# A decode block with attention on one core: wo in 48 rows per partition, read behind the last V, with attention outputs placed by selector matmuls, batch outermost and q by columns

## The chip, the cores and the metric

One core of one Trainium2 chip runs the kernel. The metric is the device time of one execution in microseconds (us); lower is better. The engines are PE (TensorE, matmuls; PEld is its weight load), DVE (VectorE), ACT (ScalarE), POOL (GpSimd) and SP (SyncE, which here only issues DMA transfers). A trace of one execution with its profile was taken for every kernel. Times in the profile count from the span's start; the timed runs are longer than the span.

A ratio below is the mean time of one kernel's fast runs over that of the other's of the same rounds, so it is not quite the ratio of the medians that are quoted.

## The reference, cut to what matters

One decode step for four sequences: layer norm, attention over a cache of 4096 positions with 32 heads of 192 values, then a gated feed-forward layer.

```python
B, Sq, D = 4, 1, 640
Hq, Hkv, Sk, Dh = 32, 32, 4096, 192          # every head has its own K and V
F = 1536
q = layernorm(x) @ wq                         # wq [640, 6144]
scores = einsum("bhqd,bhkd->bhqk", q, k_cache) * Dh ** -0.5
o = einsum("bhqk,bhkd->bhqd", softmax(scores), v_cache)
h = x + o.reshape(B, Sq, Hq * Dh) @ wo        # wo [6144, 640]
g = silu(layernorm(h) @ w_gate); u = layernorm(h) @ w_up
out = h + (g * u) @ w_down
# ... all inputs bf16
```

K and V are 201 MB each. They are read once and hardly reused, so the reading is the job.

## The kernel before

The work is cut into 32 units of one batch and four heads. Per unit there is one K of 6.29 MB and one V of 6.29 MB, each read by one DMA transfer with one contiguous run of 49152 bytes per partition. The engines work in order: four DVE products of K with q (`tt`), four PE sums (`red`), four DVE sums (`rsum`), the maximum, the exponentials on ACT; the PV matmuls of the unit before are put in front of the last `red`.

```python
def src(a, u):
    c, b = u // B, u % B                      # heads outermost, batch innermost
    return a[b, 4 * c:4 * c + 4].rearrange("h (q t) d -> (h q) (t d)", t=T)

def load_k(u):                                # two K slots
    deps = [lambda: tk["tt", u - 2, NQ - 1]] if u >= 2 else ([wq_used] if u == 1 else [])
    ...
VP = [(0, 64), (64, 96), (96, 112), (112, T)] # the last V comes in four pieces
def load_v(u):                                # one V slot: waits for the PV before
    deps = [(lambda: tk["pv", u - 1]) if u >= 1 else wq_used]
    ...
# one SP queue: wq, K0, K1, V0, K2, V1, K3, ..., K31, V30, wo_a, V31, wo_b, wg, wu, wd
def load_wo(lo, hi, t, deps):                 # three rows of 1280 bytes: runs of 3840 bytes
    a = dma("sp", lambda e: e.dma_start(
        t[:, :, :, :].rearrange("q p j n -> q p (j n)"),
        wo[lo * 2 * DH:hi * 2 * DH, :].rearrange("(p q j) n -> q p (j n)", q=128, j=3)), ...)
# ...
def o_t(u):                                   # transposes one unit's output: 6 fp32 matmuls
    for j in range(3):
        for s in range(2):
            lo = XO.start + 2 * j
            op("pe", lambda e, j=j, s=s, lo=lo: e.matmul(
                psL[64 * s:64 * s + 64, lo:lo + 2], lhsT=orow[:, j:DH:3], rhs=pick[:, s:4:2], ...))
# ... otm divides by the softmax sum; the 144 matmuls of wo_a run before the last PV
```

Of the kernel before, what the change touches and what calls it, by code (L numbers as in the profile page):

```python
# [12 lines left out]

LOOPS = True
FASTQ = False
LATE = True
SPLITU = True
XONE = False
AHEAD = False
# [17 lines left out]
class Prog:  # L37
# [33 lines left out]
    def roll(self, eng, first, last):  # L71
        self.rolled[eng] = (first, last)
# [14 lines left out]
    def emit(self, block, final):  # L87
# [24 lines left out]
        def run(eng):  # L112
            def body(e):
                ops, waits = self.ops[eng], self.waits(eng)
                if AHEAD and eng in ("dve", "act"):
                    e.addr_align(bass.FETCH_BLOCK_INSTRUCTIONS, offset=64, max_nops=0)
                i = 0
                if eng in self.rolled:
                    first, last = self.rolled[eng]
# [21 lines left out]
                    with self.nc.Fori(0, count, 1, engines=bass.OrderedEngineSet([e.engine]),  # L141
                                      head_slot={e.engine: 0} if eng == "pe" else None) as s:
                        self.shift = s
                        for j in range(n):
                            for k, v, d in plan[j]:
                                e.wait_ge(k, s * d + v)
                            one(e, ops[a + j])
                        self.shift = 0
# [39 lines left out]
def build_kernel(nc: bass.Bass, cfg: Cfg, x, kc, vc, wq, wo, wg, wu, wd, out):  # L188
# [4 lines left out]
    P = H // 2  # L193
    NU = (H // 4) * B
# [3 lines left out]
    J = DH // R  # L198
    QS = 2.0 ** -4
    alpha = 1.0 / (QS * math.sqrt(DH))  # L200
    assert B == 4 and DH == 192 and D == 640 and F == 1536 and P == 16 and T == 128 and QT * R == 512
# [16 lines left out]
    OTall = sb("OTall", [128, NU, 2, 3], BF16)  # L218
    qsb = sb("qsb", [128, 4, 2 * DH], BF16)
    sel = sb("sel", [128, B, 128 if FASTQ else 32], BF16)  # L220
    identF = sb("identF", [128, 128], FP32)
    identH = sb("identH", [128, 128], FP16)
    identB = sb("identB", [128, 128], BF16)
    halfm = sb("halfm", [128, 128], FP32)
# [6 lines left out]
    xrow = x4 = sb("x4", [B, D], BF16) if XONE else sb("xrow", [128, DQ], BF16)  # L231
# [8 lines left out]
    lsb = sb("lsb", [128, 2], FP32)  # L240
    invL = sb("invL", [128, 2], FP32)
# [11 lines left out]
    assert at(vslot) - at(kslot[1]) == SLOT and at(prod[1]) - at(prod[0]) == SLOT // 4  # L253
    WA = 12
    wqsb = nc.alloc_sbuf_tensor_at("wq_sb", [128, CD, H * DH], BF16, offset=at(kslot[1]))
    woA = nc.alloc_sbuf_tensor_at("wo_a", [128, WA, 3, D], BF16, offset=at(kslot[0]))
    woB = nc.alloc_sbuf_tensor_at("wo_b", [128, P - WA, 3, D], BF16, offset=at(prod[0]))
# [5 lines left out]
    psR, psS, psO, psH, psL = PB[0:4], PB[4], PB[5], PB[6], PB[7]  # L263
    psQ = [PB[7], PB[3]]
    XT, XB, XL, XO = slice(0, 128), slice(128, 132), slice(0, 2), slice(4, 10)
# [6 lines left out]

    if XONE:
        xd = [dma("act", lambda e: e.dma_start(x4[:, :], x[:, 0, :]), S_x)]
    else:
        xd = [dma("act", lambda e, n=n: e.dma_start(xrow[32 * n:32 * n + B, :], x[:, 0, n * DQ:(n + 1) * DQ]), S_x)
              for n in range(4)]
# [10 lines left out]
    c3 = op("pool", lambda e: e.memset(halfm[:, :], 0.0), [c2])  # L288
    for r in range(4):
        c3 = op("pool", lambda e, r=r: e.memset(halfm[32 * r:32 * r + 32, 64 * (r % 2):64 * (r % 2) + 64], 1.0), [c3])  # L290
    c4 = op("pool", lambda e: e.memset(ones_row[:, :], 1.0), [c3])
    c4 = op("pool", lambda e: e.memset(lsb[:, :], 0.0), [c4])
    pool_done = op("pool", lambda e: e.memset(pbuf[:, :, :], 0.0), [c4])

    if not XONE:
        zx = op("dve", lambda e: e.memset(xrow[:, :], 0.0))
        for t in xd:
            t.deps.append(zx)
    zp = None
    for k in (6, 0, 1, 2, 3, 5):  # L300
        zp = op("dve", lambda e, k=k: e.memset(PB[k][:, 0:2 * DH], 0.0))
    op("dve", lambda e: e.memset(epsv[:, :], eps))
    if FASTQ:
        ksel = op("dve", lambda e: e.tensor_copy(
            out=sel[:, :, :].rearrange("q b (h i) -> q b h i", h=4),
            in_=identF[:, :].rearrange("q (h r) -> q r h", h=4)[:, 0:B, :, None].broadcast_to([128, B, 4, 32])), [c2])
    else:
        ksel = op("dve", lambda e: e.tensor_copy(
            out=sel[:, :, :], in_=r32[:, 0:B][:, :, None].broadcast_to([128, B, 32])), [c1])
# [5 lines left out]
    kidb = op("dve", lambda e: e.tensor_copy(out=identB[:, :], in_=identF[:, :]), [c2])  # L315
# [21 lines left out]
    if XONE:  # L337
        for n in range(4):
            a = op("pe", lambda e, n=n: e.matmul(psH[32 * n:32 * n + B, 0:DQ], lhsT=identB[0:B, 0:B],
                                                 rhs=x4[:, n * DQ:(n + 1) * DQ], start=True, stop=True), [kidb, zp] + xd)  # L340
        ln1 = layer_norm(psH[:, 0:DQ], [a])
    else:
        ln1 = layer_norm(xrow[:, :], xd)
        for n in range(4):
            op("pe", lambda e, n=n: e.matmul(psH[32 * n:32 * n + B, 0:DQ], lhsT=identB[:, 32 * n:32 * n + B],
                                             rhs=xrow[:, :], start=True, stop=False), [kidb, zp] + xd)
# [5 lines left out]
    if FASTQ:  # L352
        for c in range(CD):
            for k in range(4):
                for n in range(4):
                    rhs = wqsb[:, c, 8 * k * DH:8 * (k + 1) * DH].rearrange("q (s d) -> q s d", s=2)[:, :, n * DH:(n + 1) * DH]
                    mm = partial(held_matmul, size=(128, 32), position=(0, 32 * n)) if k else lambda e, *a, **kw: e.matmul(*a, **kw)
                    a = op("pe", lambda e, k=k, c=c, n=n, rhs=rhs, mm=mm: mm(
                        e, PB[k][32 * n:32 * n + B, 0:2 * DH], lhsT=lnT[:, c, 0:B], rhs=rhs,
                        start=(c == 0), stop=(c == CD - 1)), [ln1, wq_land, zp])  # L360
                if c == CD - 1:
                    qcopy.append(op("act", lambda e, k=k: e.activation(
                        out=qsb[:, k, :], in_=PB[k][:, 0:2 * DH], func=ACTF.Copy, scale=1.0), [a]))
    else:
        for k in range(4):
            for c in range(CD):
                for n in range(4):
                    p = 2 * (4 * (k // 2) + n) + k % 2
                    a = op("pe", lambda e, k=k, c=c, n=n, p=p: e.matmul(  # L369
                        PB[k][32 * n:32 * n + B, 0:2 * DH], lhsT=lnT[:, c, 0:B],  # L370
                        rhs=wqsb[:, c, p * 2 * DH:(p + 1) * 2 * DH], start=(c == 0), stop=(c == CD - 1)),
                        [ln1, wq_land, zp])
            qcopy.append(op("act", lambda e, k=k: e.activation(
                out=qsb[:, k, :], in_=PB[k][:, 0:2 * DH], func=ACTF.Copy, scale=1.0), [a]))
    wq_used = a

    def src(a, u):
        c, b = u // B, u % B
        return a[b, 4 * c:4 * c + 4].rearrange("h (q t) d -> (h q) (t d)", t=T)
# [8 lines left out]
    VP = [(0, 64), (64, 96), (96, 112), (112, T)]  # L388

    def load_v(u):  # L390
        deps = [(lambda: tk["pv", u - 1]) if u >= 1 else wq_used]
        if u < NU - 1:
            landed["v", u] = [dma("sp", lambda e: e.dma_start(  # L393
                vslot[:, :, :].rearrange("q t d -> q (t d)"), src(vc, u)), S_v, deps)]
        else:
            s = src(vc, u).rearrange("q (t d) -> q t d", d=DH)
            landed["v", u] = [dma("sp", lambda e, lo=lo, hi=hi: e.dma_start(vslot[:, lo:hi, :], s[:, lo:hi, :]),
                                  sem(f"s_v{lo}"), deps) for lo, hi in VP]
# [3 lines left out]
    for u in range(NU - 1):  # L402
        load_v(u)
        if u + 2 < NU:
            load_k(u + 2)
    wo_land = {}

    def load_wo(lo, hi, t, deps):
        a = dma("sp", lambda e: e.dma_start(
            t[:, :, :, :].rearrange("q p j n -> q p (j n)"),  # L410
            wo[lo * 2 * DH:hi * 2 * DH, :].rearrange("(p q j) n -> q p (j n)", q=128, j=3)), sem(f"s_wo{lo}"), deps)
        for p in range(lo, hi):
            wo_land[p] = a

    load_wo(0, WA, woA, [lambda: tk["tt", NU - 2, NQ - 1]])
    if LATE:
        load_v(NU - 1)
    load_wo(WA, P, woB, [lambda: tk["red", NU - 1, NQ - 1]])
    if not LATE:
        load_v(NU - 1)  # L420
# [4 lines left out]
    for lo, hi in ((0, 3), (3, CD)) if SPLITU else ((0, CD),):  # L425
# [12 lines left out]
    qbc = {}  # L438
    if FASTQ:
        for i in range(NU // 2):  # L440
            k, b, bank = i // B, i % B, psQ[i % 2]
            a = op("pe", lambda e, bank=bank, k=k, b=b: e.matmul(
                bank[:, 0:2 * DH], lhsT=sel[:, b, :], rhs=qsb[:, k, :], start=True, stop=True),
                [qcopy[k], qcopy[-1], ksel, qbc.get(i - 2)])
            qbc[i] = op("act", lambda e, k=k, b=b, bank=bank: e.activation(
# [119 lines left out]
    for u in range(NU):  # L565
# [12 lines left out]
        if u >= 1:  # L578
            stt(u - 1)
# [113 lines left out]
```

## Time and profile before

The time before was 991.96 us (median of 3 runs, 991.73 to 992.19).

| what | reading |
|---|---|
| busy share of the span | PE 59%, DVE 56%, ACT 11%, DMA queue q1 99.5% |
| bytes read | 424.29 MB |
| rate in the middle | 433 GB/s |
| rate while wo_a is read | 407 GB/s |
| last K usable | 924.54 us |
| last piece of wd usable | 986.91 us |
| end | 990.1 us |

These are the lines of the page: span, busy time of the engines, the DMA queue, and the chain of work that ended last by line.

```profile
span 990.1 us, 9773 instructions
PE 581.2 (59%) x4656; PEld 117.9 (12%) x3248; DVE 552.5 (56%) x451; ACT 108.7 (11%) x348; POOL 3.4 (0%) x19
...
q1 hardware_dynamic: 12752, 424.29, 99.5%
```

The queue is busy for all but 0.5% of the span, so a gain has to come from shorter work on the queue, or from queue time that is lost at the ends.

The windows view gives, for a stretch of time, the busy time of each engine, the granted PE clock, the share of the DMA engines and the rate in GB/s. The first two are stretches of two units in the middle; the third lies inside the reading of wo_a.

```profile
core 0: us, PE busy (x) PEld busy (x) DVE busy (x) ACT busy (x) POOL busy (x), PEclk, DMA share, GB/s
110.49:168.57 58.08, 34.74 (x260) 6.51 (x172) 33.93 (x26) 5.79 (x20) 0.00 (x0) 0.79 1.00 433
865.53:923.61 58.08, 35.01 (x260) 6.51 (x172) 33.94 (x26) 5.79 (x20) 0.00 (x0) 0.79 1.00 433
938.00:950.00 12.00, 8.46 (x101) 2.93 (x83) 5.05 (x8) 3.08 (x11) 0.00 (x0) 0.96 1.02 407
```

The small packets of wo cost 6% of the rate. The share of 1.02 is the sum of the packets' durations, and above 1.00 it says that the durations overlap.

The timeline has start, duration, engine, line and operation; in brackets the idle time before it and what ended it. These two lines mark where the last K has landed (DVE starts on it) and where the last piece of wd has landed (PE loads weights for the last down matmuls).

```profile
924.54 6.63 DVE L468 TENSOR_TENSOR prod<-k,qball 128x6144 f16<-128x6144 bf16 x2 [5.92 <-DMA k<-in_A_k_cache_dram]
...
986.91 0.10 PEld L632 LDWEIGHTS pb<-wd_sb,guT 128*4 128x4 bf16 x8 [0.43 <-DMA wd_sb<-in_B_w_down_dram]
```

I call the time up to the first line the head and the middle, and from the first to the second, 986.91 - 924.54 = 62.37 us, the tail. What is left to the end is 3.2 us.

### The profile page before, as it was taken

The page shows a single profiled execution, that of the slowest core. Times are in us where ns is not written, and L with a number is a line of the kernel's source. Part 1 is how long each engine was busy: PE and PEld are TensorE (multiplying, and loading weights), DVE is VectorE, ACT ScalarE, POOL GpSimd, SP SyncE. Part 2 cuts the span into 40 slices and gives each one's busy share as a digit, 9 for nine tenths or more (in the row PEclk, how much of TensorE's full clock was granted, in tenths as well). Part 3 has the DMA queues.
Part 4 walks back from the last instruction along what each step waited for, and adds up shares of the span by engine and source line. Part 5 has one row for each costly group of instructions (what it writes and reads, how often), then busy time and mean ns, then how long its engine had stood idle before and what let it go on. Part 6 is the DMA issues. An engine that isn't in the chain of part 4 may idle for free.

```text
span 990.1 us, 9773 instructions
## 1 busy us (share of the span) xinstructions
PE 581.2 (59%) x4656; PEld 117.9 (12%) x3248; DVE 552.5 (56%) x451; ACT 108.7 (11%) x348; POOL 3.4 (0%) x19
## 2 busy tenths in 40 slices
PE   0876655666555576555557655555665555666564
PEld 0100111110101111001111100111110011110031
DVE  1486655566645556664555666455666555566602
ACT  0311111110011110001111001111100111100011
POOL 1000000000000000000000000000000000000000
PEclk9797778887777888777788877788887778887765
DMA  9999999999999999999999999999999999999998
GB/s 407 418 443 432 422 445 429 429 445 417 441 435 423 445 429 429 445 419 439 435 423 445 429 429 445 421 437 435 423 445 429 429 445 421 437 433 425 423 417 333
DMA packets 12810, 424.43 MB, mean 429 GB/s; under 512 B 1280, under 2 KB 1280, under 8 KB 4096
## 3 DMA queue, kind: packets, MB, share of 16 engines
q1 hardware_dynamic: 12752, 424.29, 99.5%
q8 instruction: 7, 0.11, 0.0%
q14 instruction: 3, 0.02, 0.0%
q10 hardware_dynamic: 48, 0.01, 0.0%
HBM read 424.29 MB, written 0.01 MB: 429 GB/s over the span
## 4 chain that ended last, share of the span: by engine, by line
DMA 64%; PE 19%; DVE 12%; SPq 2%; issue 1%; ACT 0%; DVEq 0%; ACTq 0%
DMA k<-in_A_k_cache_dram 59%; PE pb L168 12%; DVE prod L468 12%; PE pb L520 4%; DMA wd_sb<-in_B_w_down_dram 2%; DMA xrow<-in_A_x_dram 2%; PE pb L476 2%; SPq L432 1%; PE pb L369 1%; SPq L426 1%; SPq L393 0%; PE pb L456 0%; DVE sc L481 0%; ACT qball L460 0%; SPq L422 0%
## 5 line engine op out<-in xcount | busy, mean ns | idle before, releaser
L468 DVE TENSOR_TENSOR prod<-k,qball 128x6144 f16<-128x6144 bf16 x128 | 426.3, 3351 | 195.6 <-DMA k<-in_A_k_cache_dram 195.6
L168 PE MATMUL pb<-prod,identH 128*128 128x512 f16 x1408 | 385.4, 430 | 0.0
L476 PE MATMUL pb<-prod,identH 128*128 128x512 f16 x128 | 57.7, 450 | 338.2 <-DVE prod L468 330.2
L481 DVE TENSOR_REDUCE sc<-pb 128x32 f32<-128x512 f32 x128 | 88.0, 688 | 111.8 <-PE pb L168 111.8
L520 PE MATMUL pb<-v,pbuf 128*8 128x384 bf16 x2048 | 91.8, 332 | 2.7 <-DMA v<-in_A_v_cache_dram 2.5
L526 ACT ACTIVATE otmp<-pb,mask 128x192 f32<-128x192 f32 x32 | 13.5, 421 | 671.4 <-PE pb L520 671.4
L476 PEld LDWEIGHTS pb<-prod,identH 128*128 128x128 f16 x128 | 13.2, 103 | 585.2 <-DVE prod L468 472.6
L509 ACT ACTIVATE pbuf<-sc,negM 32x128 bf16<-32x128 f32 x128 | 73.4, 574 | 4.9
L520 PEld LDWEIGHTS pb<-v,pbuf 128*8 128x8 bf16 x2048 | 46.8, 87 | 115.6 <-DMA v<-in_A_v_cache_dram 59.8
L530 DVE SCALAR_TENSOR_TENSOR orow<-pb,mask,otmp 128x192 f32<-128x192 f32 x32 | 13.4, 418 | 74.0 <-ACT otmp L526 74.0
L509 ACT ACTIVATION_READ_ACCUMULATOR pbuf<-sc,negM 32x1 f32 x128 | 31.7, 248 | 0.0
L545 PE MATMUL pb<-pick,orow 128*64 128x2 f32 x384 | 22.3, 231 | 2.8 <-DVE orow L530 1.0
L503 ACT ACTIVATE negM<-pb 128x4 f32<-128x4 f32 x32 | 5.6, 174 | 156.9 <-PE pb L499 156.9
L535 PEld LDWEIGHTS pb<-lsb,halfm 128*128 128x128 f32 x64 | 12.3, 194 | 72.1 <-issue 71.1
L545 PEld LDWEIGHTS pb<-pick,orow 128*64 128x64 f32 x384 | 19.6, 174 | 6.2 <-DVE orow L530 1.7
L499 PE MATMUL pb<-negMc,ones_row 1*128 1x4 f32 x64 | 12.2, 258 | 11.8 <-DVE negMc L494 11.8
L494 DVE TENSOR_REDUCE negMc<-pb 1x4 f32<-1x128 f32 x32 | 8.9, 278 | 15.1 <-PE pb L490 15.1
L490 PE MATMUL pb<-identF,msb 128*1 128x128 f32 x64 | 12.1, 270 | 8.3 <-DVE msb L486 8.2
L323 PE MATMUL pb<-mv,quadm 128*128 128x2 f32 x4 | 1.2, 363 | 23.7 <-DVE mv L321 23.7
L499 PEld LDWEIGHTS pb<-negMc,ones_row 1*128 1x128 f32 x64 | 9.4, 182 | 21.2 <-DVE negMc L494 21.2
L319 DVE BATCH_NORM_STATS2 stats<-xrow 128x6 f32<-128x160 bf16 x1 | 0.3, 327 | 17.7 <-DMA xrow<-in_A_x_dram 17.7
L559 PE MATMUL pb<-wo_a,OTall 128*4 128x160 bf16 x144 | 5.3, 336 | 7.7 <-DMA wo_a<-in_A_wo_dram 6.3
(66 smaller groups left out, 95.8 us busy)
## 6 DMA issues: line engine op xcount, KB each, us to landing
k<-in_A_k_cache_dram SPq DMA_DIRECT2D x32, 6144.0 KB, 39.6
v<-in_A_v_cache_dram SPq DMA_DIRECT2D x31, 6144.0 KB, 25.5
wq_sb<-in_A_wq_dram SPq DMA_DIRECT2D x1, 7680.0 KB, 21.3
wo_a<-in_A_wo_dram SPq DMA_DIRECT2D x1, 5760.0 KB, 39.2
v<-in_A_v_cache_dram SPq DMA_DIRECT2D x1, 3072.0 KB, 18.4
wo_b<-in_A_wo_dram SPq DMA_DIRECT2D x1, 1920.0 KB, 28.0
wg_sb<-in_B_w_gate_dram SPq DMA_DIRECT2D x1, 1920.0 KB, 32.2
v<-in_A_v_cache_dram SPq DMA_DIRECT2D x1, 1536.0 KB, 21.8
```

Of the source, the lines that this page charges most:

```text
L168: return e.add_instruction(mybir.InstMatmult(name=e.bass.get_next_instruction_name(), engine=mybir.EngineType.PE, start_tensor_calc=start, ...
L468: op("dve", lambda e: e.tensor_tensor(out=prod[BUF[k]][:, :, :], in0=kslot[u % 2][:, k * QT:(k + 1) * QT, :], in1=qball[:, bass.ds(u + 2 * ...
L476: op("pe", lambda e, j=j: (e.matmul if j == 0 else partial(held_matmul, e))(psR[k][:, 0:QT * R], lhsT=identH[:, :], rhs=prod[BUF[k]][:, :, ...
L481: op("dve", lambda e: e.tensor_reduce(sc[u % 2][:, k * QT:(k + 1) * QT], psR[k][:, 0:QT * R].rearrange("q (t r) -> q t r", r=R), AX.X, ALU ...
L490: op("pe", lambda e: e.matmul(psS[0:1, XT], lhsT=msb[:, 0:1], rhs=identF[:, :], start=True, stop=True), [g("rmax", u), g("negM", u - 1), p ...
L499: op("pe", lambda e: e.matmul(psS[:, XB], lhsT=ones_row[0:1, :], rhs=negMc[0:1, :], start=True, stop=True), [g("hmax", u), g("negM", u - 1 ...
L509: op("act", lambda e, h=h, r=r: e.activation(out=pbuf[r, :, h], in_=sc[u % 2][r, :], func=ACTF.Exp, bias=negM[r, h:h + 1], scale=alpha, ac ...
L520: op("pe", lambda e, t=t, n=n: e.matmul(psO[32 * n:32 * n + 8, 0:2 * DH], lhsT=pbuf[:, t:t + 2, :].rearrange("q t m -> q (t m)"), rhs=vslo ...
L526: op("act", lambda e: e.activation(out=otmp[:, :], in_=psO[:, 0:DH], func=ACTF.Copy, scale=mask[:, 0:1]), [g("pv", u), g("stt", u - 1), km ...
L530: op("dve", lambda e: e.scalar_tensor_tensor(out=orow[:, :], in0=psO[:, DH:2 * DH], scalar=mask[:, 1:2], in1=otmp[:, :], op0=ALU.mult, op1 ...
L535: op("pe", lambda e: e.matmul(psL[:, XL], lhsT=halfm[:, :], rhs=lsb[:, :], start=True, stop=True), [g("exp", u), g("otm", u - 1)], key=("l ...
L545: op("pe", lambda e, j=j, s=s, lo=lo: e.matmul(psL[64 * s:64 * s + 64, lo:lo + 2], lhsT=orow[:, j:DH:3], rhs=pick[:, s:4:2], start=True, s ...
```

## The change

The intent: read wo in long runs; put it behind the last V, so that the last PV and what follows it hide behind the reading of wo; make the attention output in the layout that this needs (row 48 q + j of wo on partition q); produce q sooner. Batch goes outermost so that the outputs of one batch fill one group of 48 columns of a PSUM bank.

The diff, cut to its core:

```diff
-        c, b = u // B, u % B
+        b, c = u // NC, u % NC
...
+    def vsrc(u):
+        return vslot if u < NU - 1 else kslot[0]      # the last V goes to a free K slot
...
-    load_wo(0, WA, woA, [lambda: tk["tt", NU - 2, NQ - 1]])
-    if LATE:
-        load_v(NU - 1)
-    load_wo(WA, P, woB, [lambda: tk["red", NU - 1, NQ - 1]])
+    for lo, hi, deps in ((0, 36, [lambda: tk["pv", NU - 2]]), (36, JW, [lambda: tk["red", NU - 1, NQ - 1]])):
+        t = dma("sp", lambda e, lo=lo, hi=hi: e.dma_start(
+            wosb[:, lo:hi, :], wo[:, :].rearrange("(q j) n -> q j n", j=JW)[:, lo:hi, :]), sem(f"s_wo{lo}"), deps)
...
     def o_t(u):
-        for j in range(3):
-            for s in range(2):
-                ...                                   # six fp32 matmuls, then otm on DVE
+        for i in range(NI):                           # NI = 4, JW = 48
+            op("pe", lambda e, i=i: e.matmul(
+                psT[:, bass.ds(JW * at_unit(u)[0], JW)], lhsT=here[:, NI - 1 - i:NI - 1 - i + 128],
+                rhs=orow[:, JW * i:JW * (i + 1)], start=False, stop=(i == NI - 1), skip_group_check=True), ...)
...
-    xd = [dma("act", ...) for n in range(4)]
+    xd = dma("act", lambda e: e.dma_start(x16[:, :], x[:, 0, :].rearrange("b (n d) -> (b n) d", n=4)), S_x)
...                                                   # q: 80 matmuls, 64 on held weights; 12 copies instead of 16
+                if eng == "pe":
+                    e.addr_align(bass.FETCH_BLOCK_INSTRUCTIONS, offset=0, max_nops=0)
...
-    pr.roll("pe", 1 if FASTQ else 2, NU)              # PE's loop starts at unit 2
+    pr.roll("pe", 1, NU, 1)                           # PE's loop starts at unit 1
```

The softmax sum now comes before PV and its reciprocal is folded into the masks (`minv`), so `otm` is gone. `here` is a copy of a shifted selector, made per unit on ACT.

## The prediction

> **What bounds the kernel now.** The DMA queue. The busy table gives PE 59%, DVE 56%, ACT 11% of the 990.1 us span; the queue table gives q1 99.5% of all 16 engines' time. In 58.08 us stretches from 110 to 923 us (two K and two V of 6.29 MB each) the windows view reads 432 to 433 GB/s every time. The Trainium skill, "DMA: Bandwidth & Descriptors", section "Where 436 GB/s comes from", puts the ceiling at 435.2 GB/s; the trace agrees to half a per cent. At 433 GB/s all 424.29 MB take 980 us, so only 10 us are anything else: about 2 us before the first packet, 3.2 us after the last wd piece lands (986.9), the rest slower bytes at both ends.
>
> **Steady state.** The waits view of SP shows V waiting up to 29.1 us for the previous PV, but another transfer is in flight meanwhile: near the end PV 30 is done at 942.2 while wo_a keeps the queue busy until 953.4, so some 11 us are to spare. The change moves l_sum ahead of PV, replaces 6 small fp32 matmuls by 4 wider ones, adds an ACT copy (here) and a DVE product (minv), drops otm: under 2 us per unit on engines that idle about 40%. Worth 0. Batch outermost only reorders equal contiguous reads: 0.
>
> **Head.** x lands at 21.9 us, behind wq. Layer norm, 80 q matmuls (6.2 us) and 16 copies (8.4 us) follow. But K0 lands only at 36.5, and K1 is issued at 31.7, before the queue runs dry. The faster q (one x transfer, held weights, 12 copies for 16) shortens work with 4 us to spare: 0 to 0.3 us.
>
> **Tail, where the gain is.** wo goes in 3840-byte packets now: the windows view falls to 407 GB/s over 938 to 950 us. By the trace's DMA records such a packet takes 153.8 ns, one of 49152 bytes 1819.6, one of 15360 bytes 578.6. So:
> - wo now: 2048 x 153.8 / 16 engines = 19.7 us. After: 128 rows of 46080 bytes (estimate at the K packets' 27.0 B/ns: 1706 ns) and 128 of 15360: (1706 + 578.6) x 8 = 18.3 us. Gain 1.4 us.
> - The last V in four pieces: 14.9 us; whole: 14.6. Gain 0.3 us.
>
> Both are on the queue that bounds, so I count all 1.7 us. After the last V, 13.8 MB follow instead of 7.9, so PV, the selector matmuls and the copy (about 8 us) hide behind wo. The 192 wo matmuls now run after it: 144 take 5.0 us at half clock against 4.6 us that the second wo piece takes, so layer norm 2 starts about 0.5 us later against the queue's end. Gate, up and down still wait for wu and wd. The end of wd to the end of the program stays 3.2 us.
>
> **Predicted:** 990.3 us, 80% range 989.2 to 991.8. Faster by over 2%: 0.5%; within 2%: 97.5%; slower by over 2%: 2%.
>
> **What would show it right or wrong.** Queue share near 99.5%, middle windows at 432 to 433 GB/s; wo near 430 GB/s; the chain still ends with K, then wd; the span 1.7 us shorter, all of it after the last K. Wrong if: middle stretches fall under 430 GB/s (order of addresses, or PV over 10 us later); K1 is issued after K0 lands; or the last down matmuls no longer wait for wd, because the wo matmuls delay layer norm 2 by over 1 us.

## More of the kernel before

The groups view gives busy time, mean ns of one, and the idle time of the engine before the group with what ended it. This is the DVE product with K:

```profile
L468 DVE TENSOR_TENSOR prod<-k,qball 128x6144 f16<-128x6144 bf16 x128 | 426.3, 3351 | 195.6 <-DMA k<-in_A_k_cache_dram 195.6
```

Over 32 units the DVE waits 195.6 / 32 = 6.1 us per unit for K. That is the room that the chain of compute of a unit has before it sets the pace.

## The result, and the profile after

The changed kernel took 990.41 us (median of 4 runs, 989.84 to 990.54) against 992.08 us for the kernel before in the same rounds (991.73 to 992.5): a ratio of 0.9982, with a 95% interval from 0.9965 to 0.9999. The same kernel again gave 990.3 us and a ratio of 0.9978 (0.9964 to 0.9992). That is the same within 2%, some 1.7 to 2.2 us shorter.

The page after, same lines as before:

```profile
span 988.3 us, 9469 instructions
PE 579.3 (59%) x4409; PEld 129.0 (13%) x2941; DVE 553.3 (56%) x454; ACT 117.1 (12%) x376; POOL 3.7 (0%) x18
...
q1 hardware_dynamic: 10528, 424.29, 99.5%
```

The bytes are the same, the packets 17% fewer. The windows view of the kernel after, two stretches in the middle, and the stretch in which the kernel before was reading wo_a; here it is the last V that lands:

```profile
110.49:168.57 58.08, 34.29 (x252) 7.39 (x164) 33.86 (x27) 6.42 (x22) 0.00 (x0) 0.79 1.00 433
865.53:923.61 58.08, 34.65 (x252) 7.38 (x164) 33.92 (x26) 6.41 (x22) 0.00 (x0) 0.79 1.00 432
938.00:950.00 12.00, 8.33 (x95) 3.87 (x81) 4.42 (x10) 3.81 (x11) 0.00 (x0) 0.91 1.00 430
```

The middle is unchanged. A rate over so short a stretch is coarse where packets are long (a packet of 46080 bytes takes 1.7 us of its engine), so I don't read one off for wo after the change; the tail as a whole is the safer measure. Its two marks, in the timeline after:

```profile
924.00 6.63 DVE L412 TENSOR_TENSOR prod<-k,qball 128x6144 f16<-128x6144 bf16 x2 [6.23 <-DMA k<-in_A_k_cache_dram]
...
985.08 0.10 PEld L571 LDWEIGHTS pb<-wd_sb,guT 128*4 128x4 bf16 x8 [0.39 <-DMA wd_sb<-in_B_w_down_dram]
```

The last piece of wd is usable 986.91 - 985.08 = 1.83 us sooner. Of these, 0.54 us were won before the last K had landed, and the tail went from 62.37 to 985.08 - 924.00 = 61.08 us, 1.29 us less. The end after the last wd is still 3.2 us, and PE still waits for wd there.

The experiments take these two numbers apart. The same two marks in every trace (one execution each; the kernels named b_ are the kernel before with an edit, those named a_ the kernel after with one):

| kernel | last K usable, us | tail, us | median, us (range) | ratio to before (95%) |
|---|---|---|---|---|
| before (profile above) | 924.54 | 62.37 | 992.31 (991.9 to 992.93) | |
| after, again (a_again) | 923.91 | 61.26 | 990.3 (989.94 to 990.32) | 0.9978 (0.9964 to 0.9992) |
| b_wo_wide | 924.58 | 61.31 | 990.93 (990.62 to 992.51) | 0.9989 (0.9976 to 1.0003) |
| a_wo_3840 | 924.02 | 62.11 | 991.4 (990.85 to 991.84) | 0.9990 (0.9976 to 1.0004) |
| a_wo_1280 | 924.04 | 64.53 | 993.34 (993.32 to 993.95) | 1.0011 (0.9997 to 1.0025) |
| b_v_whole | 925.00 | 62.16 | 991.77 (991.08 to 992.93) | 0.9996 (0.9983 to 1.0008) |
| a_v_four | 923.86 | 61.47 | 990.6 (990.48 to 990.83) | 0.9986 (0.9972 to 0.9999) |
| b_batch_outer | 924.99 | 62.34 | 991.95 (991.67 to 993.21) | 0.9999 (0.9986 to 1.0012) |
| b_head | 926.00 | 62.36 | 993.74 (991.76 to 994.28) | 1.0010 (0.9998 to 1.0022) |
| a_no_align | 925.49 | 61.07 | 991.36 (990.37 to 993.01) | 0.9995 (0.9982 to 1.0009) |
| b_head_align | 923.89 | 62.37 | 991.59 (991.3 to 992.16) | 0.9997 (0.9984 to 1.0011) |
| a_pe_few | 923.81 | 61.27 | 990.27 (989.84 to 990.44) | 0.9981 (0.9968 to 0.9995) |
| a_pe_busy | | | 1028.6 (1028.07 to 1029.76) | 1.0367 (1.0353 to 1.0380) |

The kernels came in three calls of four; the fast runs of the kernel before had medians of 992.31, 991.97 and 991.82 us there (9, 11 and 9 runs), in the second and third call with single runs up to 994.46 and 993.84. Single times of effects under 1 us are weak evidence by themselves, and most of the intervals above touch 1; the traces' marks and the times together carry the argument. The two marks repeat well: in the six traces with the change's head as it is, the last K is usable at 923.81 to 924.04 us, and in the four with the head of the kernel before at 924.54 to 925.00.

### The profile page after: what moved, and what is told of

It reads as the page before. It is cut to its first block, busy times and chain, and to the rows that moved or that the text cites. A ratio compares the mean times of both kernels' runs of the same rounds, so it can differ in the third digit from the quotient of the medians.

```text
span 988.3 us, 9469 instructions
## 1 busy us (share of the span) xinstructions
PE 579.3 (59%) x4409; PEld 129.0 (13%) x2941; DVE 553.3 (56%) x454; ACT 117.1 (12%) x376; POOL 3.7 (0%) x18
## 4 chain that ended last, share of the span: by engine, by line
DMA 67%; PE 18%; DVE 12%; issue 1%; SPq 1%; DVEq 0%
DMA k<-in_A_k_cache_dram 63%; DVE prod L412 12%; PE pb L161 11%; PE pb L462 4%; DMA wd_sb<-in_B_w_down_dram 4%; PE pb L420 2%; SPq L365 0%; DVE sc L425 0%; PE pb L468 0%; DVEq L412 0%; SPq L391 0%; SPq L385 0%; PE pb L571 0%; SPq L330 0%; PE pb L434 0%
## 5 line engine op out<-in xcount | busy, mean ns | idle before, releaser
L412 DVE TENSOR_TENSOR prod<-k,qball 128x6144 f16<-128x6144 bf16 x128 | 426.3, 3351 | 220.9 <-DMA k<-in_A_k_cache_dram 220.9
L477 ACT ACTIVATE otmp<-pb,minv 128x192 f32<-128x192 f32 x32 | 13.4, 420 | 650.8 <-PE pb L462 650.8
L462 PE MATMUL pb<-v,pbuf 128*8 128x384 bf16 x1984 | 86.0, 326 | 0.0
L481 DVE SCALAR_TENSOR_TENSOR orow<-pb,minv,otmp 128x192 f32<-128x192 f32 x32 | 13.4, 418 | 55.1 <-ACT otmp L477 55.1
L497 PEld LDWEIGHTS pb<-orow,here 128*128 128x128 f32 x256 | 33.5, 192 | 73.7 <-issue 71.1
L497 PE MATMUL pb<-orow,here 128*128 128x48 f32 x256 | 31.7, 267 | 1.1 <-DVE orow L481 1.1
L468 PEld LDWEIGHTS pb<-lsb,headm 128*128 128x128 f32 x64 | 12.3, 194 | 74.8 <-issue 71.2
L434 PE MATMUL pb<-identF,msb 128*1 128x128 f32 x64 | 12.1, 270 | 9.8 <-DVE msb L430 9.8
L468 PE MATMUL pb<-lsb,headm 128*128 128x1 f32 x64 | 9.2, 213 | 2.7 <-ACT pbuf L453 2.7
L490 ACT ACTIVATE here<-place 128x131 f32 (+1 forms) x32 | 10.0, 312 | 0.9
L430 DVE TENSOR_REDUCE msb<-sc 128x1 f32<-128x128 f32 x32 | 9.1, 286 | 1.1
```

The source lines that it names most:

```text
L412: op("dve", lambda e: e.tensor_tensor(out=prod[BUF[k]][:, :, :], in0=kslot[u % 2][:, k * QT:(k + 1) * QT, :], in1=qball[:, bass.ds(u + pr. ...
L434: op("pe", lambda e: e.matmul(psS[0:1, XT], lhsT=msb[:, 0:1], rhs=identF[:, :], start=True, stop=True), [g("rmax", u), g("negM", u - 1), p ...
L462: op("pe", lambda e, t=t, n=n: e.matmul(psO[32 * n:32 * n + 8, 0:2 * DH], lhsT=pbuf[:, t:t + 2, :].rearrange("q t m -> q (t m)"), rhs=vsrc ...
L468: op("pe", lambda e: e.matmul(psS[:, XL], lhsT=headm[:, :, :].rearrange("q r m -> q (r m)"), rhs=lsb[:, :], start=True, stop=True), [g("ex ...
L477: op("act", lambda e: e.activation(out=otmp[:, :], in_=psO[:, 0:DH], func=ACTF.Copy, scale=minv[:, 0:1]), [g("pv", u), g("minv", u), g("st ...
L481: op("dve", lambda e: e.scalar_tensor_tensor(out=orow[:, :], in0=psO[:, DH:2 * DH], scalar=minv[:, 1:2], in1=otmp[:, :], op0=ALU.mult, op1 ...
```

## The experiments

### The yardstick

> The changed kernel once more, as the yardstick on this chip. Theory (the gain is queue time: wo in wide rows 1.4 us, the last V whole 0.3 us): 1.5 to 2.0 us under the kernel before. Rival (head, order of batches or the PE work): the same total, so this run alone tells nothing apart.

Measured 2.0 us under the kernel before by medians (990.3 against 992.31), at the upper end of what was expected.

### wo in long runs, alone

The kernel before, with wo's order changed in memory only. The numbers that come out of attention are wrong. (The comparison with the reference still passed for this and all kernels with a changed order here: with these inputs the attention's part of the output is evidently too small for the tolerance to see. "Correct" proves little about wo in this problem.)

```diff
-            t[:, :, :, :].rearrange("q p j n -> q p (j n)"),
-            wo[lo * 2 * DH:hi * 2 * DH, :].rearrange("(p q j) n -> q p (j n)", q=128, j=3)), ...)
+            t[:, :, :, :].rearrange("q p j n -> q (p j) n"),
+            wo[:, :].rearrange("(q j) n -> q j n", j=3 * P)[:, 3 * lo:3 * hi, :]), ...)
```

> The kernel before with one thing changed: wo is read as 48 contiguous rows per partition (36 and 12), wrong result on purpose. Theory: packets of 3840 bytes vanish, wo takes 18.3 instead of 19.7 us of the queue, the time falls by 1.4 us (1.2 to 1.6). Rival (the gain is made in the head, by the order of batches or by fewer PE instructions): no change, within 0.3 us.

Measured: 1.4 us less by medians, 1.1 by means (991.29 against 992.41). The last K came as before (924.58), and the tail lost 1.06 us. The windows view over the stretch where the kernel before showed 407 GB/s and a share of 1.02:

```profile
938.00:950.00 12.00, 8.16 (x100) 2.93 (x83) 4.75 (x8) 3.38 (x11) 0.00 (x0) 0.93 1.00 433
```

wo in long runs is worth about 1.1 us by itself, with none of the rest of the change.

### wo in short runs again

The kernel after, with the short runs back (wrong):

```diff
-            wosb[:, lo:hi, :], wo[:, :].rearrange("(q j) n -> q j n", j=JW)[:, lo:hi, :]), ...)
+            wosb[:, lo:hi, :].rearrange("q (p j) n -> q p (j n)", j=3),
+            wo[128 * lo:128 * hi, :].rearrange("(p q j) n -> q p (j n)", q=128, j=3)), ...)
```

> The changed kernel with wo read in runs of 3840 bytes again, two transfers as now, wrong result on purpose. Theory: 2048 packets of 153.8 ns return, 1.4 us of the gain are lost: 0.3 us under the kernel before. Rival: the gain of 1.7 us stays whole.

Measured: 1.1 us over the kernel after (991.4 against 990.3), and a tail of 62.11 against 61.26, 0.85 us more. The direction and the place are right, the size is under 1.4 us.

### The suspected cost made larger

As above, but with runs of 1280 bytes (`wo[128 * lo:128 * hi, :].rearrange("(j q) n -> q j n", q=128)`). Its output is wrong, which doesn't matter for the time.

> The suspected cost amplified: the changed kernel with wo in runs of 1280 bytes, wrong result on purpose. A line through the packets of 3840 and 49152 bytes (12.6 ns + 0.0368 ns per byte) gives 59.7 ns for 1280 bytes: 6144 x 59.7 / 16 = 22.9 us against 18.3, so 4.6 us over the changed kernel (3.5 to 6). Rival: packets of wo don't matter, no change.

Measured: 3.0 us over the kernel after by medians, 3.3 by means, and 64.53 - 61.26 = 3.27 us in the tail: a miss of the expected 3.5 to 6. The packets themselves took just what was expected. The trace's DMA records (not a view of the profile; size, count, mean ns, sum over 16 engines):

```
 3840 bytes x 2048, mean 153.8 ns, 19.69 us    kernel before
46080 bytes x  128, mean 1710.3 ns, 13.68 us   kernel after
15360 bytes x  256, mean 578.7 ns,  9.26 us    kernel after (wo's second part and wg)
 1280 bytes x 6144, mean  60.1 ns, 23.07 us    a_wo_1280
49152 bytes x 8192, mean 1819.3 ns, 931.47 us  kernel after (K and V)
```

By these sums wo would cost 23.07 - (13.68 + 4.63) = 4.8 us more; 3.3 us were lost. The windows view of a_wo_1280 says why:

```profile
955.00:970.00 15.00, 4.37 (x73) 2.71 (x69) 1.53 (x4) 0.42 (x1) 0.00 (x0) 0.61 1.07 363
```

The share is 1.07: short packets overlap, so the sum of their durations is more than the time they take. The rate of 363 GB/s is the honest number. The same overlap, 1.02, lies over wo in the kernel before. Counting in the DMA records how long more than 16 packets were under way at once, from 915 us on (worked out by me, in us of all 16 engines, without the 4-byte packets that only signal completion):

```
overlap after 915 us: before 0.67, b_wo_wide 0.28, after 0.21, a_wo_3840 0.59, a_wo_1280 1.59
```

The 4.8 us of the sums, less 1.59 - 0.21 = 1.4 us of overlap, are 3.4 us: the measured loss. For 3840 bytes the 1.4 us of the sums less about 0.4 us are 1.0 us. With the overlap taken off, the sums agree with the measured tails (3.27 us, and 0.85 to 1.06 us) within 0.15 us.

### The last V in one transfer, in the kernel before

```diff
-    VP = [(0, 64), (64, 96), (96, 112), (112, T)]
+    VP = [(0, T)]
```

> The kernel before with the last V in one transfer, right result. The queue saves 0.3 us, but all of the last PV (5.1 us at half clock) then runs after V has landed, and only 1.97 MB of wo stand behind it: layer norm 2 starts about 3 us later and the chain through gate, up and down ends about 1.2 us later than today. Theory: 0.5 to 1.5 us slower. Rival (only the queue's packets count): 0.3 us faster.

Measured: 0.2 us less by medians, a tail of 62.16 against 62.37. My theory missed: I expected a loss. The 64 last PV matmuls took 4.04 us, not 5.1, then the 48 matmuls of wo_b 1.20 us instead of 1.77; layer norm 2 started at 975.44, only 0.6 us later than before, and PE still waited for wu and wd. The four pieces were bought in the kernel before for a delay that hid anyway. These lines of b_v_whole show the last PV, the wo_b matmuls and the start of layer norm 2:

```profile
968.47 4.04 PE L520 MATMUL pb<-v,pbuf 128*8 128x384 bf16 x64 [7.13 <-DMA v<-in_A_v_cache_dram]
974.11 1.20 PE L559 MATMUL pb<-wo_b,OTall 128*4 128x160 bf16 x48
975.44 0.27 DVE L319 BATCH_NORM_STATS2 stats<-pb 128x6 f32<-128x160 f32 x1
```

### The last V in four transfers, in the kernel after

The mirror: the last V's one transfer becomes the four pieces of the kernel before, and each PV matmul waits for its own piece.

> The changed kernel with the last V in four transfers again, right result. Theory: the queue loses 0.3 us by packets and 0 by compute, since all of wo stands behind it: 0 to 0.3 us slower than the changed kernel. Rival (wo behind a whole V is what makes the gain): 0.7 us or more slower.

Measured: 0.3 us over a_pe_few, which is as fast as the kernel after (990.6 against 990.27), and a tail 0.2 us longer (61.47 against 61.27). Taken with b_v_whole, the whole V is worth 0.2 to 0.3 us. But a part of that isn't queue time: the timed run is 1.76 to 1.85 us longer than its span in every kernel with the V in four pieces, and 1.53 to 1.64 us in every one with it whole. So about 0.2 us of the gain in time lie outside the span; what takes them isn't shown. Inside the span, the medians differ by 0.1 us here and by nothing in b_v_whole, while the tails of the single traces say 0.2 us.

### The order of the batches

The kernel before with `b, c = u // (H // 4), u % (H // 4)` in `src`. Its output is wrong, which doesn't matter for the time.

> The kernel before with the K and V units read batch outermost, wrong result on purpose. Theory: the same contiguous reads of 6.29 MB in another order, no change, within 0.3 us, middle stretches at 432 to 433 GB/s. Rival (reading the caches straight through is kinder to memory): at least 1 us faster.

Measured: a ratio of 0.9999, and the tail is that of before (62.34). The order of reading is worth nothing here.

### The head, without and with an aligned instruction stream

The kernel before has switches for one x transfer and for q by columns:

```diff
-FASTQ = False
+FASTQ = True
...
-XONE = False
+XONE = True
```

> The kernel before with its own switches for one x transfer and q by columns turned on, right result. Theory: x and q are done earlier, but K0 lands as before at about 36.5 us and the queue never runs dry: no change, within 0.3 us. Rival (the gain is made in the head): 1 us or more faster.

Measured: no gain, and six runs in two groups: 991.76 and 991.87, and four from 993.4 to 994.28. I had expected nothing; both theories missed. The trace (of a run of 993.4) shows two things. First, PE's timeline at the first pass of its loop, in unit 1: DVE's product was finished at 60.2 us (a start at 56.86 and 3.35 us), but the sum starts at 63.45. Then SP's timeline where the second V is issued, and the windows view just after it:

```profile
63.45 0.60 PE L476 MATMUL pb<-prod,identH 128*128 128x512 f16 x1 [6.09 <-issue]
...
77.80 0.33 SPq L393 DMA_DIRECT2D v<-in_A_v_cache_dram  x1
...
76.00:79.00 3.00, 3.00 (x51) 0.92 (x37) 1.11 (x3) 0.42 (x1) 0.00 (x0) 1.00 0.68 295
```

Until that V is issued, only the rest of K2 is in the queue. Here it comes so late that the queue is served at 295 GB/s for 3 us. The last K was usable at 926.00 us instead of 924.54.

Idle engines are not all of the loss: by the DMA records, packets of 49152 bytes that started between 79 and 82 us took up to 2.8 us instead of 1.8, which costs about another 0.65 us of all 16 engines.

In the kernel before the loop starts at unit 2, and the same stall of 3 us stands there (PE starts at 87.51 us with a product finished at about 84.5):

```profile
75.18 0.33 SPq L393 DMA_DIRECT2D v<-in_A_v_cache_dram  x1
...
87.51 0.60 PE L476 MATMUL pb<-prod,identH 128*128 128x512 f16 x1 [7.45 <-issue]
```

There it does no such harm: the next V is issued at 102.17 us, with 8 us of K3 still to come (that K is usable at 110.63), where the stalled b_head has some 3 us of K2 left at 77.80 (in b_head_align, below, that K is usable at 80.59). The diff has one line that I had passed over, `addr_align` for PE. Taking it out of the kernel after, and putting it into b_head:

```diff
 # a_no_align: the kernel after
-                if eng == "pe":
-                    e.addr_align(bass.FETCH_BLOCK_INSTRUCTIONS, offset=0, max_nops=0)
 # b_head_align: b_head
+                if eng == "pe":
+                    e.addr_align(bass.FETCH_BLOCK_INSTRUCTIONS, offset=0, max_nops=0)
```

> The changed kernel without its new line that aligns the tensor engine's instruction stream to a fetch block, right result. Revised theory, after the head of the kernel before with q by columns came out 0 to 2.3 us slower: without the line the tensor engine stalls about 3 us at the first entry to its loop, in unit 1; the second V is then issued at about 77.5 instead of 74.5 us, the queue nearly runs dry before K2 has landed, and 0.5 to 2 us of the gain are lost, with more spread from run to run. Rival (the q part of the change by itself does no harm, the 0 to 2.3 us were chance): no change, within 0.3 us of the changed kernel.

> The kernel before with one x transfer, q by columns and, new, the aligned instruction stream, right result. Revised theory: the stall at the loop's entry is gone, the second V is issued at about 74.5 us, the loss of 0 to 2.3 us without the alignment vanishes: 0 to 0.7 us under the kernel before, and steadier from run to run. Rival (q by columns itself costs time): still 1 us or more above.

Measured for a_no_align: 991.36 us, about 1.1 us over a_pe_few (990.27, which is as fast as the kernel after), with a range of 2.6 us. The stall is there, V is issued at 78.26 us, and the queue sags. (The bracket names DVE here, but its product was done at about 60.5 us.)

```profile
63.74 0.60 PE L418 MATMUL pb<-prod,identH 128*128 128x512 f16 x1 [6.11 <-DVE prod L410]
...
78.26 0.33 SPq L363 DMA_DIRECT2D v<-in_A_v_cache_dram  x1
...
76.00:79.00 3.00, 3.00 (x60) 1.19 (x49) 1.50 (x5) 0.42 (x1) 0.00 (x0) 1.00 0.64 279
```

Measured for b_head_align: 991.59 us, 0.2 us under the kernel before, with a range of 0.9 us. No stall, V at 75.12 us, and the queue full:

```profile
60.81 0.61 PE L476 MATMUL pb<-prod,identH 128*128 128x512 f16 x1 [2.89 <-DVE prod L468]
...
75.12 0.33 SPq L393 DMA_DIRECT2D v<-in_A_v_cache_dram  x1
...
76.00:79.00 3.00, 2.70 (x25) 1.07 (x16) 0.98 (x2) 0.00 (x0) 0.00 (x0) 1.00 0.99 426
```

So q by columns with an aligned stream makes the last K usable 0.65 us sooner (923.89 against 924.54), and without alignment 1.5 us later (926.00). One line turns the stall, the late V and the sagging queue on and off, in both kernels: that the alignment does this is shown. (In time it is less sharp: two of the six runs of b_head were fast without it, and none of these was traced.) Engines that had nothing to do between 70 and 84 us, and the instruction queue's packets of 16384 bytes in the first 900 us, from the DMA records (a reckoning, not a view; us):

```
                idle 70 to 84   instruction packets, start (each about 1.0 long)
before          0.00            37.1, 44.6, 84.9, 92.0
after           0.00            1.9, 60.7
b_head          0.63            60.9, 67.8
a_no_align      0.73            61.2, 68.0
b_head_align    0.00            2.0, 62.1
```

The table also says what the 0.54 and 0.65 us are not. In the kernel before, the kernel after and b_head_align no engine idled, and that V is issued at 75.18, 74.50 and 75.12 us: the late V explains what the missing alignment costs, not what the head wins over the kernel before. What differs there is the instruction packets, which take time on the same 16 engines. Following each engine's packets through the records, the 16 engines finish the last K at 922.36 us in mean and the slowest at 923.91 in the kernel before; after the change these are 922.17 and 923.35. So 0.19 us of the difference are in the mean, and 0.37 us are in how far the slowest engine, which a transfer has to wait for, lies behind it; in the kernel before that engine had carried the packet of 84.9 us. Three packets of 1.0 us, each on one of 16 engines, are of that size. The size fits, but no run tested this by itself.

In the three kernels without alignment a block of instructions is fetched inside the stall (84.9 in 84.5 to 87.5; 60.9 and 61.2 in 60.2 to 63.7). In the aligned ones a block comes at about 2 us instead, long before it is needed, and PE starts without waiting. That the stall is a fetch is thus well supported, though no view names it. The Trainium skill, "Runtime: NRT & Kernel Launch", section "Instruction fetch mechanics", says that instructions come in blocks of 16 KiB through a DMA queue of the sequencer, and that a taken branch out of the blocks at hand has to wait for a fetch. The 16384-byte packets agree with the first. That the loop's entry is such a branch isn't shown; the page gives no duration for the wait, and the stalls here took 3.0 to 3.3 us.

### How much room a unit has

The kernel after with more copies of the softmax-sum matmul in front of PV, in all units but the last:

```diff
+    EXTRA = 19            # 6 in the second kernel
...
+        for _ in range(extra):
+            op("pe", lambda e: e.matmul(psS[:, XL], lhsT=headm..., rhs=lsb[:, :], start=True, stop=True), ...)
```

> The changed kernel with 19 more copies of the softmax-sum matmul in front of each PV but the last, about 0.43 us each, some 8 us per unit, 250 us of PE work in all, right result. Theory (a unit has about 11 us to spare before the queue runs dry): no change, within 0.5 us. Rival (the tensor engine's work per unit is on the path): tens to 250 us longer.

> The changed kernel with 6 instead of 19 more copies of the softmax-sum matmul per unit, right result. Revised theory: a unit's chain through DVE and PE has about 6.9 us to spare (the DVE's mean wait for K), 19 copies with PV at half clock took about 7.5 us and ran over it; 6 copies take 1.6 us, with PV at half clock at most 4 us: no change, within 0.5 us of the changed kernel. Rival (PE work per unit counts in proportion): 6/19 of 38 us, 12 us longer.

Measured: 19 copies cost 38 us, 6 cost nothing. The first expectation was wrong, because its 11 us of room were wrong. The group of the DVE product, in the kernels after, a_pe_busy and a_pe_few, in that order of fences:

```profile
L412 DVE TENSOR_TENSOR prod<-k,qball 128x6144 f16<-128x6144 bf16 x128 | 426.3, 3351 | 220.9 <-DMA k<-in_A_k_cache_dram 220.9
```

```profile
L413 DVE TENSOR_TENSOR prod<-k,qball 128x6144 f16<-128x6144 bf16 x128 | 426.0, 3347 | 30.0 <-DMA k<-in_A_k_cache_dram 26.2 <-issue 3.7
```

```profile
L413 DVE TENSOR_TENSOR prod<-k,qball 128x6144 f16<-128x6144 bf16 x128 | 426.4, 3352 | 180.5 <-DMA k<-in_A_k_cache_dram 180.4
```

In the kernel after DVE waits for K 220.9 / 32 = 6.9 us per unit: that is the room. With 19 copies it is used up, and the unit I looked at takes 30.64 us (products start at 419.47 and 450.11 us in the timeline) against 29.04 us of queue; 38 us over 31 units are 1.2 us each. The copies took some 5 us, and PV after them 5.16 us instead of 2.77:

```profile
409.89 5.16 PE L463 MATMUL pb<-v,pbuf 128*8 128x384 bf16 x64
```

```profile
938.69 2.77 PE L462 MATMUL pb<-v,pbuf 128*8 128x384 bf16 x64
```

PE's granted clock was lower there: 0.53 over this PV and 0.50 over that of the next unit, against 1.00 over a PV of 2.77 us in the kernel after (windows view). The Trainium skill, "TensorE: Matmul & The Clock Gate", section "What's actually happening", names two states of the clock, full rate and half rate; the trace's clocks and its 2.77 and 5.16 us for the same 64 matmuls agree. Why the clock fell just after the copies, in which PE was busy, isn't shown. With 6 copies 5.6 us of the room are left and the time stays.

So the serial chain of DVE and PE within a unit, not the transfers in flight, sets the limit; the queue was the bound only because that chain had 6.1 us to spare before the change, and 6.9 after. (The room grew by 0.8 us per unit and bought nothing.)

## Why the prediction was right or wrong

The time (990.3 predicted, 990.41 and 990.3 measured), the class and the place of most of the gain were right. That the sum came within 0.1 us is partly luck, because it was better than its terms:

- **The queue bounds, the middle doesn't move: right.** 432 to 433 GB/s before and after; b_batch_outer and a_pe_few cost nothing.
- **"some 11 us are to spare": wrong.** The step read the room off one transfer in flight. The waits of DVE for K gave 6.1 us before, 6.9 after, and a_pe_busy, 7 to 8 us more per unit, was 38 us slower. The conclusion "worth 0" stood because the change made the chain shorter, not longer.
- **wo, "Gain 1.4 us": right in kind, too large.** Measured 0.85 to 1.1 us, alone and undone. The failed step is the sum of packet durations: short packets overlap (share 1.02 over wo, 1.07 with 1280 bytes), by 0.46 us more before than after. Taken from the windows view instead, 7.86 MB at 407 GB/s (the kernel before) and at 433 (b_wo_wide, the same stretch) are 19.3 and 18.2 us: 1.2 us.
- **The whole last V, "Gain 0.3 us": right in size**, 0.2 to 0.3 us, but in part by luck: the step counted queue time only, and about 0.2 us of the gain in time lie outside the span.
- **Head, "0 to 0.3 us", and "all of it after the last K": wrong.** 0.54 us of the gain lie before the last K. The step looked for work that comes too late for the queue, and K0 and K1 are indeed issued in time; in the kernel before the queue doesn't run dry near 75 us either. What it left out is the instruction fetches on the same DMA engines: four blocks between 37 and 92 us before, one after the change (argued from the records, not tested). And the gain is there only because of the alignment of PE's instructions, which the prediction didn't mention and without which the head costs about 1.5 us in the trace: that was luck.
- **"layer norm 2 starts about 0.5 us later against the queue's end": wrong in sign, without effect.** Counted back from the last landing of wd it started 986.91 - 974.82 = 12.1 us earlier before, 985.08 - 972.64 = 12.4 after. All 192 matmuls of wo took 5.92 us in one go, 31 ns each, where 35 ns had been assumed.
- **The 3.2 us after wd: right.**

The tail gained 1.29 us instead of 1.7, the head 0.54 instead of at most 0.3, and about 0.2 us came outside the span, where nothing had been expected: the misses cancelled. What stays open: why single runs of the kernel before lie up to 2.8 us above its fastest while all 9 timed runs of the kernel after lie within 0.7 us. The queue sagging near 75 us is a candidate, since the kernels with the late V (b_head, a_no_align) spread too, and b_v_whole and b_batch_outer, which have the head of the kernel before, show 0.16 and 0.10 us of idle engines there and the last K at 925.0; but no slow run of the kernel before itself was traced.

No experiment pointed to a kernel that beats both by more than the noise. Each part of the change that pays is already in it.

## What to carry to other kernels

When a DMA queue is full, cost a change by the rate in a window, not by summed packet durations, and look for the moments when only part of one transfer is queued: there a 3 us delay on another engine costs queue time. A full queue isn't the end of it: a transfer is usable when its slowest DMA engine is done, so look at what else those engines carry. Read the room of the compute chain from the wait for data at its first engine (here DVE for K), because in-order engines form one serial chain. When a loop's entry moves, compare the first pass of the loop in both traces; an instruction stream can stall there without any wait in the program.

## What the Trainium skill lacked or had wrong

- "DMA: Bandwidth & Descriptors", section "Specifications", gives 512 bytes as the smallest transfer for line rate. Here runs of 3840 bytes were read at 407 GB/s and of 1280 bytes at 363, against 433 for runs of 49152.
- The same page, section "Where 436 GB/s comes from", says that for transfers between HBM and SBUF the HBM side binds, with about 358 GB/s (the stack's 716 divided by two cores), beside its own measurement of 425. This core, with no other running the kernel, read 433 GB/s over the middle of its span; the section's other limit, 435.2, was the one that fitted.
- The same page, section "Queues, rings and completion order", says that an engine takes turns between its queue rows packet by packet. The traces agree; what the page lacks is how long a turn can be. In the kernel before, x came in four transfers, and the DMA records show four chains of eight small packets, one after each packet of wq (61440 bytes, 2.27 us): the last started at 21.47 us, and x was usable at 21.9. In the kernel after, x is one transfer, sixteen chains of two such packets, and was there at 8.5 us.
- "Runtime: NRT & Kernel Launch", section "Instruction fetch mechanics", has no duration for a taken branch that must fetch, nor that aligning the stream to its blocks can help: 3.0 to 3.3 us of stall at the first entry of PE's loop (well supported as a fetch, not proven), gone with one alignment. Nor does it say what a fetch takes from the DMA engines that carry the data: about 1.0 us of one engine for each block of 16384 bytes.
- No page says by how much the durations of short DMA packets in a trace overlap: their sum was 1.02 of the time at 3840 bytes and 1.07 at 1280.
